# The first layer's up product of the last batch by Strassen's algorithm, its weight sums made one batch earlier

## Chip, cores and metric

One core of a Trainium2 chip runs the whole program. The metric is the device time of one execution in microseconds (us). Its engines are PE (TensorE, matrix products), DVE (VectorE), ACT (ScalarE), POOL (GpSimd) and SP (SyncE, which here only issues DMAs).

## The reference

Three stages are fused, each fed by the one before.

```python
# 1 linear attention: batch 4, heads 8, S 576, head width 64
q_p, k_p = phi(q), phi(k)
num = einsum('bhsf,bhfd->bhsd', q_p, einsum('bhsf,bhsd->bhfd', k_p, v))
x = num / (einsum('bhsf,bhf->bhs', q_p, k_p.sum(2))[..., None] + 1e-06)   # as 2304 x 512
# 2 first layer: w_in 512 x 2048, w_out 2048 x 512
h = x @ w_in
x = np.maximum(0.01 * h, h) @ w_out
# 3 second layer: 4 experts, w1 512 x 1024, w2 1024 x 512
out = sum(p[:, e:e+1] * (np.maximum(x @ w1[e], 0) @ w2[e]) for e in range(4))
```

The change touches `h = x @ w_in`, for the last of the four batches (576 of the 2304 rows).

## The kernel before

Every float32 operand of a matrix product is split in two parts, high and low (`hilo`, L120 to L125: ACT casts the high part, DVE subtracts it from the source and keeps the rest). A product takes three passes, high with high, high with low and low with high:

```python
    PASS = ((0, 0), (0, 1), (1, 0))
```

**The first layer.** Batches 0 to 3 are worked one after the other. The attention of batch b leaves x^T as KK = 4 tiles of 128 x 576 (`xh`, `xl`). The 2048 columns of w_in are taken 128 at a time: F counts these pieces through all batches, 16 per batch (NF), so batch 3 is F = 48 to 63. `moe1_up(F, n)` makes one half n (288 of the 576 columns) of piece F with 4 x 3 = 12 matmuls (L530). After both halves the gate follows: ACT writes 0.01 h (`hs`, L542), DVE takes the maximum (`g`, L544), ACT casts it (`gt`, L124), DVE makes its low part (L125). `moe1_down(C, d, n)` multiplies the four gated pieces of a group by w_out: 4 x 3 matmuls for each half n of each of the four output tiles d (L563). DVE adds the result to `acc` (L576); the first group of a batch is copied by ACT instead (L574).

**The order.** A group G holds GF = 4 pieces, so batch 3 is groups 12 to 15. In a group, ups of this group and downs of the one before alternate:

```python
ORDER = (("u", 0), ("d", 0), ("d", 1), ("u", 1), ("d", 2), ("d", 3), ("u", 2), ("u", 3))
```

Each "u" is 24 matmuls, each "d" 24. The order of the other work comes from a plan of steps with fractional batch times (`plan`, sorted). A scheduler then sets the order on each engine, save where the code calls `keep_in_program_order`. From the second batch on, weights are read back from float32 copies in DRAM: `w1_dma` loads a raw tile `wr` (128 x 512, 4 buffers), `w1_split` makes `wt` from it.

**What else runs in batch 3.** The second layer is already worked by Strassen's algorithm, in two blocks of tokens. `x2_steps(0)` and `x2_steps(1)` prepare its inputs from the finished batches: POOL makes differences (`xt`, L665), ACT casts (`xo`, L683), POOL subtracts (`xo`, L685), SP stores halves of them in DRAM (L692). `early()` loads `w1[1]` and `w2[0]` ahead. At the end of batch 3 SP loads `r`, the first expert's weights (L733), POOL makes their sums (`rs`, L747), ACT casts (`wuh`, L772) and POOL subtracts (`wul`, L777). Then PE starts the second layer's products (L849).

## Time and profile before

| What | Value |
|---|---|
| Median of 3 runs | 1342.0 us (1339.99 to 1342.63) |
| The profiled execution, its own time | 1342.56 us |
| Its span in the trace | 1340.8 us |
| PE busy | 1315.7 us (98%) |
| DVE, ACT, POOL busy | 69%, 48%, 49% |
| Up matmuls (L530), whole run | 1536, of which batch 3 has 384 |
| Batch 3's first layer, from F = 48 to the last `acc` | 502.7 to 618.9 us |

The trace has one row for each instruction or run of like instructions. A matmul's record is longer than the pace at which matmuls follow, because they overlap in the array; the pace is read from a run of them in the chain of waits.

### The profile page before, as it was taken

The page shows a single profiled execution, that of the slowest core. Times are in us where ns is not written, and L with a number is a line of the kernel's source. Part 1 is how long each engine was busy: PE and PEld are TensorE (multiplying, and loading weights), DVE is VectorE, ACT ScalarE, POOL GpSimd, SP SyncE. Part 2 cuts the span into 40 slices and gives each one's busy share as a digit, 9 for nine tenths or more (in the row PEclk, how much of TensorE's full clock was granted, in tenths as well). Part 3 has the DMA queues.
Part 4 walks back from the last instruction along what each step waited for, and adds up shares of the span by engine and source line. Part 5 has one row for each costly group of instructions (what it writes and reads, how often), then busy time and mean ns, then how long its engine had stood idle before and what let it go on. Part 6 is the DMA issues. An engine that isn't in the chain of part 4 may idle for free.

```text
span 1340.8 us, 23230 instructions
## 1 busy us (share of the span) xinstructions
PE 1315.7 (98%) x8303; PEld 1272.1 (95%) x8303; DVE 927.1 (69%) x1385; ACT 642.8 (48%) x1225; POOL 656.5 (49%) x550
## 2 busy tenths in 40 slices
PE   7979999999999999999999999999999999999998
PEld 6879999999999999999999999899999999999998
DVE  5589889877776665474666666556676667667667
ACT  5667656676666544543444444343333324332331
POOL 2223102111112103457566566278888868777775
PEclk9999999999999999999999999999999999999999
DMA  6465575433344234567999999998888899887882
GB/s 214 127 239 189 185 230 152 139 110 114 94 129 140 73 105 130 182 241 260 322 307 309 305 362 386 345 337 294 291 290 288 293 381 369 252 267 249 265 255 102
DMA packets 196850, 312.37 MB, mean 233 GB/s; under 512 B 20608, under 2 KB 96256, under 8 KB 196736
## 3 DMA queue, kind: packets, MB, share of 16 engines
q1 hardware_dynamic: 196736, 310.90, 70.4%
q8 instruction: 66, 1.08, 0.3%
q14 instruction: 48, 0.39, 0.1%
HBM read 222.04 MB, written 88.72 MB: 232 GB/s over the span
## 4 chain that ended last, share of the span: by engine, by line
PE 88%; DVE 6%; DMA 3%; issue 1%; ACT 1%; SPq 0%; DVEq 0%; ACTq 0%
PE po L1060 17%; PE op L563 13%; PE hp L530 12%; PE po L889 10%; PE py L1011 7%; PE px L1011 5%; PE pv L1011 5%; PE py L849 4%; PE kvp L258 3%; PE nm L351 3%; PE px L849 3%; PE pv L849 2%; PE pk L220 1%; DMA r<-w_in 1%; DVE gt L125 1%
## 5 line engine op out<-in xcount | busy, mean ns | idle before, releaser
L1076 DVE TENSOR_TENSOR ac<-po,ac 128x768 f32<-128x768 f32 x203 | 194.0, 956 | 123.7 <-PE po L1060 123.7
L1060 PE MATMUL po<-go,wo 128*128 128x384 f32 x1302 | 260.9, 336 | 0.0
L312 POOL PARTITION_ALL_REDUCE mb<-pc x32 | 78.0, 2440 | 347.8 <-ACT pc L310 258.6
L1060 PEld LDWEIGHTS po<-go,wo 128*128 128x128 f32 x1302 | 228.6, 188 | 0.4 <-ACT ac L1074 0.2
L563 PE MATMUL op<-gt,wt 128*128 128x288 f32 x1536 | 220.1, 297 | 1.7 <-DVE gt L125 1.5
L530 PE MATMUL hp<-xh,wt 128*128 128x288 f32 x1024 | 215.8, 297 | 1.4 <-DVE g L544 1.4
L563 PEld LDWEIGHTS op<-gt,wt 128*128 128x128 f32 x1536 | 208.1, 188 | 3.5 <-DVE gt L125 2.2
L1042 ACT CAST go<-t 128x384 fp32r<-128x384 f32 x124 | 63.8, 514 | 221.1 <-POOL t L1038 221.1
L530 PEld LDWEIGHTS hp<-xh,wt 128*128 128x128 f32 x1024 | 167.1, 188 | 2.8 <-DVE g L544 2.0
L530 PE MATMUL hp<-xl,wt 128*128 128x288 f32 x512 | 151.6, 296 | 1.8 <-DVE xl L125 1.8
L1046 POOL TENSOR_TENSOR go<-t,go 128x384 fp32r<-128x384 f32 x124 | 131.8, 1074 | 19.3 <-ACT go L1042 19.3
L889 PE MATMUL po<-wd,gh 128*128 128x512 f32 x384 | 129.8, 391 | 0.0
L1011 PE MATMUL py<-xo,wo 128*128 128x384 f32 x576 | 115.7, 336 | 0.0
L1046 POOL TENSOR_TENSOR go<-b,go 128x384 fp32r<-128x384 f32 x95 | 97.6, 1028 | 9.2 <-ACT go L1042 9.2
L1011 PEld LDWEIGHTS py<-xo,wo 128*128 128x128 f32 x576 | 101.3, 188 | 0.3
L530 PEld LDWEIGHTS hp<-xl,wt 128*128 128x128 f32 x512 | 96.1, 188 | 2.6 <-DVE xl L125 2.2
L907 DVE SCALAR_TENSOR_TENSOR ob<-po,pe,ob 128x512 f32<-128x512 f32 x90 | 67.4, 749 | 44.7 <-PE po L889 44.7
L1038 POOL TENSOR_TENSOR t<-b,b 128x384 f32<-128x384 f32 x62 | 64.0, 1032 | 62.2 <-DVE b L1031 62.2
L889 PEld LDWEIGHTS po<-wd,gh 128*128 128x128 f32 x384 | 72.0, 188 | 13.2
L125 DVE TENSOR_TENSOR wt<-wr,wt 128x512 fp32r<-128x512 f32 x96 | 72.0, 768 | 17.2 <-ACT wt L124 17.0
L1011 PE MATMUL px<-xo,wo 128*128 128x384 f32 x384 | 77.5, 337 | 0.0
L1011 PE MATMUL pv<-xo,wo 128*128 128x384 f32 x384 | 77.4, 337 | 0.0
(153 smaller groups left out, 2639.5 us busy)
## 6 DMA issues: line engine op xcount, KB each, us to landing
wo<-wu SPq DMA_DIRECT2D x224, 256.0 KB, 4.0
wo<-wx SPq DMA_DIRECT2D x124, 256.0 KB, 5.1
wo<-wp SPq DMA_DIRECT2D x97, 256.0 KB, 3.7
wr<-w SPq DMA_DIRECT2D x96, 256.0 KB, 2.8
r<-w SPq DMA_DIRECT2D x32, 512.0 KB, 5.7
wx<-ws SPq DMA_DIRECT2D x32, 512.0 KB, 5.1
wu<-wuh SPq DMA_DIRECT2D x16, 896.0 KB, 5.1
wu<-wul SPq DMA_DIRECT2D x16, 896.0 KB, 5.6
```

Of the source, the lines that this page charges most:

```text
L125: nc.vector.tensor_tensor(out=lo, in0=src, in1=hi.bitcast(F32), op=ALU.subtract)
L312: nc.gpsimd.partition_all_reduce(mb, pc, 128, bass_isa.ReduceOp.absmax)
L530: nc.tensor.matmul(hp[:, n, 0:HS], lhsT=wi[:, a, kk * 128 : (kk + 1) * 128], rhs=x[z][:, kk, n * HS : (n + 1) * HS], start=(kk == 0 and i ...
L563: nc.tensor.matmul(op[:, n, 0:HS], lhsT=wt1[1, C * GF + f][:, a, d * 128 : (d + 1) * 128], rhs=gts[C * GF + f][:, z, n * HS : (n + 1) * HS ...
L849: kept(nc.tensor.matmul(out, lhsT=ws[w][:, AOPS.index(a), kk * 128 : (kk + 1) * 128], rhs=x[z][:, kk], start=first and n == 0, stop=n == 5 ...
L889: kept(nc.tensor.matmul(op.rearrange("p (h m) -> p h m", h=2), lhsT=(gh, gl)[z][:, 2 * f + t, q : q + 128], rhs=d[:, w, f::2], start=n == ...
L907: kept(nc.vector.scalar_tensor_tensor(out=o, in0=op, scalar=ps, in1=o, op0=ALU.mult, op1=ALU.add))
L1011: kept(nc.tensor.matmul(out, lhsT=w[:, wz, kk * 128 : (kk + 1) * 128], rhs=x[z][:, kk], start=first and n == 0, stop=n == 5, skip_group_ch ...
L1038: kept(nc.gpsimd.tensor_tensor(out=t, in0=gr[k, a], in1=gr[k, b], op=ALU.subtract))
L1046: kept(eng.tensor_tensor(out=t[:, 1], in0=gr[k, name], in1=t[:, 0].bitcast(F32), op=ALU.subtract))
L1060: kept(nc.tensor.matmul(t[:, m, 0:TH], lhsT=w[:, wz, m * 128 : (m + 1) * 128], rhs=g[:, z], start=n == 0, stop=n == 2,))
L1076: kept(nc.vector.tensor_tensor(out=A[j, i], in0=src, in1=A[j, i], op=ALU.add))
```

## The change

In batch 3 (SB = 3) two pieces of w_in, a pair, are made together by Strassen's algorithm. The pair's weights are four blocks (two halves of the 512 inputs by two pieces), x^T of the batch is four blocks (two halves of the inputs by two halves of 288 columns). Seven products of 2 x 3 matmuls take the place of 48 matmuls: 42 per pair, 336 instead of 384 for the eight pairs (`pair_product`, L657 to L695 in the numbering of the changed kernel, its matmuls at L673).

What comes with it:

- Weight sums (`f_sums`, L554): in batch 2, four DVE operations of 128 x 256 per pair on the raw tiles (L564), and two DMAs that store them in DRAM (L567). In batch 3 `f_dma` (L575) loads seven forms of 128 KB per pair, `f_split` casts and subtracts each (256 columns). This replaces two loads of 256 KB and two casts and subtracts of 512 columns per pair.
- x forms (`x_mul_forms`, L407): four sums or differences and seven splits on 576 columns, where there were four splits.
- Sums of products, per pair: three ACT copies of 288 columns out of PSUM (L684, L686, L688) and two DVE adds in PSUM (L690, L693). The gate becomes one ACT leaky ReLU (L699) instead of ACT 0.01 h and DVE maximum.
- Downs of batch 3 in halves with one PSUM bank each, evicted by DVE 288 columns at a time, first group included (L806, L810).
- PE and ACT keep the program's order through batch 3 (`held`), from a list in `pair_group`. The steps of `x2_steps` go to 16 places of that list (`slot`).
- `early()` reuses the tile `xt` of `x2_steps(1)`, so its loads wait until POOL has read that tile. POOL now sums `w1[1]` before `r` (L988), and the load of `r` (L974) waits for a PE matmul 105 ahead of the next stage's first.
- POOL's first six differences (L906) wait for the last matmul of F = 47's up, whose `xl` gives their tile its place.

```diff
+SB = B - 1
+FORMS = ("a11", "s1", "s2", "a12", "s4", "s3", "a22")
+X2SLOTS = ((0,), (2, 1), (3, 5), (4,), (6, 8), (7,), (9, 10), (11,))
...
+    fwp = opened(leftw, "fwp", 7)
...
+    pin = {"on": ""}
+
+    def held(e, ins):
+        if e in pin["on"]:
+            tc.keep_in_program_order(ins)
...
+    def x_split(b, n, src):
...
+        nc.scalar.copy(out=hl[:, 0], in_=src)
+        nc.vector.tensor_tensor(out=hl[:, 1], in0=src, in1=hl[:, 0].bitcast(F32), op=ALU.subtract)
+
+    def x_mul_forms(b, hp):
...
+        if hp == 1:
+            t1 = unit("t1").rearrange("p (a s) -> p a s", a=2)
+            sub(t1, b12, b11)
+            x_split(b, "b11", b11)
+            x_split(b, "t1", t1)
+        if hp == NP - 1:
+            sub(b12, b22, b12)
+            sub(b11, b12, b11, ALU.add)
+            x_split(b, "t2", b11)
+            x_split(b, "b21", b21)
+            x_split(b, "b22", b22)
+            x_split(b, "t3", b12)
+            sub(b21, b21, b11)
+            x_split(b, "t4", b21)
...
+    def f_sums(F):
+        a, b = (raws1.pop((0, F - 1 + i)) for i in range(2))
+        t = [fwp.tile([128, 2, 256], F32, tag="fw", name="fs") for _ in range(2)]
+        s = {1: t[0][:, 0], 2: t[0][:, 1], 4: t[1][:, 0], 3: t[1][:, 1]}
+        for o, x, y, op in (
+            (1, b[:, 0:256], b[:, 256:512], ALU.add),
+            (2, s[1], a[:, 0:256], ALU.subtract),
+            (3, a[:, 0:256], b[:, 0:256], ALU.subtract),
+            (4, a[:, 256:512], s[2], ALU.subtract),
+        ):
+            nc.vector.tensor_tensor(out=s[o], in0=x, in1=y, op=op)
+        d = drw.tile([128, 4, 256], F32, name=f"fs_{F}")
+        for i in range(2):
+            nc.sync.dma_start(out=d[:, 2 * i : 2 * i + 2], in_=t[i])
...
+    def f_dma(F, a):
+        if F < B * NF:
+            t = wf[F, a] = fwp.tile([128, 2, 256], F32R, tag="fw", name="wf")
+            nc.sync.dma_start(out=t[:, 1].bitcast(F32), in_=wsum[F % NF][a]())
+
+    def f_split(F, a):
+        if F < B * NF:
+            t = wf[F, a]
+            hilo(t[:, 0], t[:, 1], t[:, 1].bitcast(F32), 'w', B)
...
+    PRODUCTS = {
+        1: ("a11", "b11"), 2: ("a12", "b21"), 3: ("s4", "b22"), 4: ("a22", "t4"),
+        5: ("s1", "t1"), 6: ("s2", "t2"), 7: ("s3", "t3"),
+    }
...
+        if F == SB * NF - 1:
+            pin["on"] = "A"
+            pair_product(F + 1, 1)
+            pin["on"] = ""
...
+    def pair_product(F, i):
...
+        for kk in range(2):
+            for wz, z in PASS:
+                held("P", nc.tensor.matmul(
...
+        if i == 1:
+            ub[F][1] = two("hp")
+            held("A", nc.scalar.copy(out=ub[F][1][:, 0, 0:HS], in_=X))
+        elif i == 5:
+            held("A", nc.scalar.copy(out=ss[:, 0], in_=V))
+        elif i == 6:
+            held("A", nc.scalar.copy(out=ss[:, 1], in_=Y))
+        elif i == 3:
+            held("V", nc.vector.tensor_tensor(out=V, in0=V, in1=ss[:, 1], op=ALU.add))
+            pair_gate(F, xv)
+        elif i == 7:
+            held("V", nc.vector.tensor_tensor(out=Z, in0=Y, in1=ss[:, 0], op=ALU.add))
+        elif i == 4:
+            pair_gate(F + 1, yz)
+
+    def pair_gate(F, t):
+        g = unit("g")
+        held("A", nc.scalar.activation(
+            out=g.rearrange("p (a s) -> p a s", a=2), in_=t[:, :, 0:HS], func=AF.Lrelu, alpha=0.01
+        ))
...
+    def pair_group(G):
...
+            if u == 0:
+                M += [
+                    P[1], f("a12="), P[4], w(F - 1), P[5], P[6], f("s4=", "s3="), d[0],
+                    f("a22=", "a11"), slot, P[2], f("s1"), d[1], f("s2"), P[3], slot, d[2], P[7],
+                    f("a12"), w(F), d[3], slot, d[4],
+                ]
+            else:
+                M += [
+                    P[1], P[4], f("s4="), w(F - 1), P[5], f("s3="), w(F), d[0], P[6], P[2],
+                    f("a22=", "a11"), d[1], f("s1"), slot, f("s2"), d[2], P[3], P[7],
+                ]
+        if (G + 1) * GF == B * NF:
+            M[-3:] = [P[3], P[7], d[2], lambda F=F: pair_product(F, 4)]
...
+        halves = "P" in pin["on"]
+        if halves:
+            op = one("op").unsqueeze(1).to_broadcast([128, 2, 512])
...
+        if c == 0 and halves:
+            held("V", nc.vector.tensor_copy(av, ov))
...
+                if F // NF == SB - 1 and F % 2:
+                    f_sums(F)
...
-                t = xp.tile([128, 3, 2, TH], F32, tag="x", name="xt")
+                if j:
+                    t = m2["early"] = accp.tile([128, 3, 2, TH], F32, tag="a", name="xt")
+                else:
+                    t = xp.tile([128, 3, 2, TH], F32, tag="x", name="xt")
...
     def early():
-        t = accp.tile([128, 2, 4, 256], F32, tag="a", name="r0")
+        t = m2["early"].rearrange("p a b c -> p (a b c)")[:, 0:2048]
...
-    plan += [(B - 0.1, lambda: r01.append(early()))]
-    plan += spread(x2_steps(0), B - 0.95, B - 0.5) + spread(x2_steps(1), B - 0.5, B - 0.05)
+    FB = SB * NF
+    plan += [(SB - 0.15 + 0.02 * i, lambda a=a: f_dma(FB, a)) for i, a in enumerate(FORMS)]
+    plan += [(SB - 0.08 + 0.02 * i, lambda a=a: f_split(FB, a)) for i, a in enumerate(FORMS[:3])]
+    plan += [(SB - 0.01, pair_feed)]
```

PE at the start of batch 3. `hp` on the left is an up, `op` a down; numbers tell the tiles apart. Before, the end of F = 48's up (`hp_5978`), then the first half down of group 11, which reads pieces 44 to 47 in turn (`gt_5850` is 47's):

```order
L530 MATMUL hp_5978<-xh_4805,wt_5855 128x288 x2
L530 MATMUL hp_5978<-xl_4806,wt_5855 128x288
L530 MATMUL hp_5978<-xh_4805,wt_5855 128x288
L563 MATMUL op_6013<-gt_5605,wt_5690 128x288 x3
L563 MATMUL op_6013<-gt_5709,wt_5789 128x288 x3
L563 MATMUL op_6013<-gt_5808,wt_5831 128x288 x3
L563 MATMUL op_6013<-gt_5850,wt_5884 128x288 x3
```

And now, from the end of F = 47's up (`hp_5905`) on: P1, P5 and P6 of the first pair, the same half down, then P2:

```order
L630 MATMUL hp_5905<-xh_3121,wt_5857 128x288
L673 MATMUL hp_5946<-xf_5220,wf_5744 128x288 x6
L673 MATMUL hp_5946<-xf_5220,wf_5777 128x288 x6
L673 MATMUL hp_5953<-xf_5843,wf_5792 128x288 x6
L792 MATMUL op_6002<-gt_5659,wt_5746 128x288 x3
L792 MATMUL op_6002<-gt_5774,wt_5879 128x288 x3
L792 MATMUL op_6002<-gt_5898,wt_5920 128x288 x3
L792 MATMUL op_6002<-gt_5957,wt_5976 128x288 x3
L673 MATMUL hp_5946<-xf_5843,wf_5820 128x288 x6
```

Between F = 47's up and the first down there were 24 matmuls, now there are 18. P5 writes the PSUM tile whose other bank P1 filled, and its first matmul waits for ACT's copy of P1.

DVE at the same place. Before, from the `g` of F = 47 on:

```order
L544 TENSOR_TENSOR g<-hp,hs 128x576 [waits Activation_49]
L125 TENSOR_TENSOR wt<-wr,wt 128x512 [waits DMAHW1_49,Activation_49]
L125 TENSOR_TENSOR gt<-g,gt 128x576 [waits Activation_49]
L125 TENSOR_TENSOR wt<-wr,wt 128x512 [waits DMAHW2_49,Activation_49]
L544 TENSOR_TENSOR g<-hp,hs 128x576 [waits Activation_49]
```

And now (`fs` are the sums of the last pair, `wf` low parts of forms; the third `fs` waits for P5's matmuls, since its tile is the buffer that P5 reads):

```order
L648 TENSOR_TENSOR g<-hp,hs 128x576 [waits Activation_49]
L564 TENSOR_TENSOR fs<-wr 128x256 [waits PE_49]
L564 TENSOR_TENSOR fs<-fs,wr 128x256 [waits DVE_49]
L564 TENSOR_TENSOR fs<-wr 128x256 [waits PE_49]
L136 TENSOR_TENSOR gt<-g,gt 128x576 [waits Activation_49]
L564 TENSOR_TENSOR fs<-wr,fs 128x256 [waits DVE_49]
L136 TENSOR_TENSOR wf<-wf 128x256 [waits DMAHW1_49,Activation_49]
L136 TENSOR_TENSOR wt<-wr,wt 128x512 [waits DMAHW3_49,Activation_49]
```

In both, the low part of `gt` of F = 47 comes first and the low part of `wt` of F = 47 later (the last `wt` row). Three sums now stand ahead of the one, and a fourth sum and a form between the two. The first half down reads both when it comes to piece 47.

SP in the middle of batch 3. Before, loads of `wr` between the stores of `xo`:

```order
L692 DMA xo_b_6543<-xo 128x768 [waits DMAHW1_49,Activation_49]
L692 DMA xo_b_6543<-xo 128x768 [waits DMAHW2_49,Pool_49]
L451 DMA wr<-w_0_13_1923 128x512 [waits DMAHW3_49,DVE_49]
L692 DMA xo_t_6633<-xo 128x768 [waits DMAHW4_49,Activation_49]
L692 DMA xo_b_6666<-xo 128x768 [waits DMAHW5_49,Activation_49]
```

And now:

```order
L933 DMA xo_b_6929<-xo 128x768 [waits DMAHW0_49,Activation_49]
L578 DMA wf<-fs_5755 128x256 [waits DMAHW1_49,PE_49]
L933 DMA xo_b_6929<-xo 128x768 [waits DMAHW2_49,Pool_49]
L578 DMA wf<-fs_5755 128x256 [waits DMAHW3_49,PE_49]
L578 DMA wf<-w_0_14_2055 128x256 [waits DMAHW4_49,DVE_49,PE_49]
L578 DMA wf<-w_0_13_1926 128x256 [waits DMAHW5_49,PE_49]
L578 DMA wf<-fs_5929 128x256 [waits DMAHW6_49,DVE_49,PE_49]
```

The loads of the forms (`wf`) stand behind stores that wait for POOL and ACT, and wait themselves for the PE product that last read their buffer.

## Rows read from the trace of the kernel before

**Rows 1.** The page's part 1: busy us, share of the span, instructions.

```profile
PE 1315.7 (98%) x8303; PEld 1272.1 (95%) x8303; DVE 927.1 (69%) x1385; ACT 642.8 (48%) x1225; POOL 656.5 (49%) x550
```

**Rows 2.** Chain of waits in batch 3: start us, us, what.

```profile
496.35 9.54 PE hp L530 x72
...
512.26 3.18 PE hp L530 x24
...
591.80 6.37 PE op L563 x48
```

**Rows 3.** Busy time by window: PE, PEld, DVE, ACT, POOL; clock, DMA share, GB/s.

```profile
440.00:480.00 40.00, 40.00 (x310) 40.00 (x309) 25.86 (x42) 20.68 (x41) 0.00 (x0) 1.00 0.30 87
560.00:600.00 40.00, 40.00 (x304) 40.00 (x303) 26.16 (x33) 18.49 (x29) 25.24 (x22) 1.00 0.61 211
```

**Rows 4.** ACT's groups, 380 to 640 us: shape, count | busy us, mean ns.

```profile
L124 ACT CAST gt<-g 128x576 fp32r<-128x576 f32 x32 | 21.6, 674 | 19.1 <-DVE g L544 19.1
L542 ACT ACTIVATE hs<-hp 128x576 f32<-128x576 f32 x32 | 20.8, 650 | 48.2 <-PE hp L530 48.1
L358 ACT COPY nf<-nm 128x288 f32<-128x288 f32 x12 | 4.7, 397 | 8.5 <-PE nm L351 8.5
```

**Rows 5.** DVE's groups, 380 to 640 us: the nearest to the new sums.

```profile
L819 DVE TENSOR_TENSOR ws<-r 128x256 f32<-128x256 f32 x4 | 1.6, 418 | 0.0
```

**Rows 6.** Timeline of DVE at F = 47: start us, us, instruction.

```profile
503.43 0.76 DVE L544 TENSOR_TENSOR g<-hp,hs 128x576 f32<-128x576 f32 x1 [0.92 <-ACT hs L542]
504.93 0.76 DVE L125 TENSOR_TENSOR gt<-g,gt 128x576 fp32r<-128x576 f32 x1
```

**Rows 7.** Timeline of DVE, low parts with POOL idle and with POOL busy.

```profile
497.11 1.89 DVE L125 TENSOR_TENSOR wt<-wr,wt 128x512 fp32r<-128x512 f32 x3
...
573.52 3.69 DVE L125 TENSOR_TENSOR wt<-wr,wt 128x512 fp32r<-128x512 f32 x3
577.13 0.74 DVE L544 TENSOR_TENSOR g<-hp,hs 128x576 f32<-128x576 f32 x1
...
578.62 1.50 DVE L125 TENSOR_TENSOR gt<-g,gt 128x576 fp32r<-128x576 f32 x1
```

**Rows 8.** Timeline of POOL, alone and in the stretch of rows 7.

```profile
518.44 1.99 POOL L685 TENSOR_TENSOR xo<-xt,xo 128x384 fp32r<-128x384 f32 x2 [6.97 <-ACT xo L683]
...
573.77 2.89 POOL L665 TENSOR_TENSOR xt<-xr,xt 128x384 f32<-128x384 f32 x2
```

**Rows 9.** Timeline of ACT: a cast that waits for DVE's result.

```profile
552.01 0.67 ACT L124 CAST gt<-g 128x576 fp32r<-128x576 f32 x1 [0.32 <-DVE g L544]
```

**Rows 10.** Timeline of PE, end of batch 3 and start of the next stage.

```profile
609.08 9.04 PE L563 MATMUL op<-gt,wt 128*128 128x288 f32 x66 [0.20 <-DVE gt L125]
...
618.97 0.61 PE L849 MATMUL px<-xo,wuh 128*128 128x384 f32 x2 [0.68 <-DVE acc L576]
...
620.13 0.52 PE L849 MATMUL pv<-xo,wuh 128*128 128x384 f32 x2
```

**Rows 11.** The page's part 6, DMA issues: count, KB each, us to landing.

```profile
wr<-w SPq DMA_DIRECT2D x96, 256.0 KB, 2.8
r<-w SPq DMA_DIRECT2D x32, 512.0 KB, 5.7
```

**Rows 12.** Timeline of POOL at the end of batch 3.

```profile
603.83 1.87 POOL L777 TENSOR_TENSOR wul<-r,wuh 128x768 fp32r<-128x768 f32 x1
...
607.68 1.94 POOL L747 TENSOR_TENSOR rs<-r 128x256 f32<-128x256 f32 x2
609.58 2.39 POOL L777 TENSOR_TENSOR wul<-rs,wuh 128x1024 fp32r<-128x1024 f32 x1
611.93 0.73 POOL L747 TENSOR_TENSOR rs<-rs,r 128x256 f32<-128x256 f32 x1
```

**Rows 13.** Timeline of SP's queue in batch 3: stores of xo that held it.

```profile
559.80 7.34 SPq L692 DMA_DIRECT2D xo_b<-xo  x2
...
585.20 12.46 SPq L692 DMA_DIRECT2D xo_t<-xo  x4
```

More of the change, by code (lines that the diff above doesn't have):

```diff
@@ L97, in opened @@
         )
-    left, left0, right, righte, leftl, psl = (ExitStack() for _ in range(6))
+    left, left0, leftw, right, righte, leftl, psl = (ExitStack() for _ in range(7))
     vp = opened(right, "vp", 2, side="right")
@@ L500, in w1_dma @@
         b, f = divmod(F, NF)
+        if i == 0 and b >= SB:
+            return
         if b == 0:
@@ L549, in moe1_up @@
         gts[F] = gt
+    ub = {}
+    def pair_product(F, i):
+        if i == 1:
+            ub[F] = [two("hp"), None, None]
+        elif i == 5:
+            ub[F][2] = unit("ss").rearrange("p (a s) -> p a s", a=2)
+        xv, yz, ss = ub[F]
+        X, V = xv[:, 0, 0:HS], xv[:, 1, 0:HS]
+        if yz is not None:
+            Y, Z = yz[:, 0, 0:HS], yz[:, 1, 0:HS]
+        out = {1: lambda: X, 2: lambda: X, 5: lambda: V, 3: lambda: V}.get(i, lambda: Y)()
+        a, b = PRODUCTS[i]
+        w, x = wf.pop((F, a)), xs[F // NF][b]
+        first = i in (1, 5)
+        n = 0
+        for kk in range(2):
+            for wz, z in PASS:
+                held("P", nc.tensor.matmul(
+                    out,
+                    lhsT=w[:, wz, kk * 128 : (kk + 1) * 128],
+                    rhs=x[z][:, kk],
+                    start=first and n == 0,
+                    stop=n == 5,
+                    skip_group_check=not first,
+                ))
+                n += 1
+        if i == 1:
+            ub[F][1] = two("hp")
+            held("A", nc.scalar.copy(out=ub[F][1][:, 0, 0:HS], in_=X))
+        elif i == 5:
+            held("A", nc.scalar.copy(out=ss[:, 0], in_=V))
[8 more added lines that the diff above has]
+            pair_gate(F + 1, yz)
@@ new lines, in pair_gate, with slot, pair_feed @@
+    def pair_gate(F, t):
+        g = unit("g")
+        held("A", nc.scalar.activation(
+            out=g.rearrange("p (a s) -> p a s", a=2), in_=t[:, :, 0:HS], func=AF.Lrelu, alpha=0.01
+        ))
+        gt = gp.tile([128, 2, S], F32R, tag="g", name="gt")
+        hilo(gt[:, 0], gt[:, 1], g, 'g', F // NF + 1)
+        gts[F] = gt
+    slots = []
+    def slot():
+        if slots:
+            for f in slots.pop(0):
+                f()
+    r01 = []
+    def pair_feed():
+        for j in range(2):
+            x = x2_steps(j)
+            slots.extend([x[i] for i in q] for q in X2SLOTS)
+        slots[-1].append(lambda: r01.append(early()))
@@ L568, in moe1_down @@
                     stop=(f == GF - 1 and i == 2),
-                )
-        if n == 0:
+                ))
+        if halves:
+            av, ov = accs[b][:, d, n * HS : (n + 1) * HS], op[:, n, 0:HS]
+        elif n == 0:
             return
-        av = accs[b][:, d].rearrange("p (a s) -> p a s", a=2)
-        if c == 0:
-            nc.scalar.copy(out=av, in_=op[:, :, 0:HS])
-        else:
-            nc.vector.tensor_tensor(out=av, in0=op[:, :, 0:HS], in1=av, op=ALU.add)
-        if c == NF // GF - 1:
+        else:
+            av, ov = accs[b][:, d].rearrange("p (a s) -> p a s", a=2), op[:, :, 0:HS]
+        if c == 0 and halves:
+            held("V", nc.vector.tensor_copy(av, ov))
+        elif c == 0:
+            held("A", nc.scalar.copy(out=av, in_=ov))
+        else:
+            held("V", nc.vector.tensor_tensor(out=av, in0=ov, in1=av, op=ALU.add))
+        if c == NF // GF - 1 and n == 1:
             nc.sync.dma_start(out=xd[b][:, d], in_=accs[b][:, d])
     def moe1_group(G):
+        if G >= SB * NF // GF and G < B * NF // GF:
+            return pair_group(G)
         def up(F, n):
```

93 lines of the change are left out of this document (80 added, 13 removed).

## The prediction, made before the changed kernel was run

> **What bounds the kernel now.** I read the page first: PE is busy 98% of the span [rows 1], so time goes down only where PE gets less work or waits less. Then the chain of waits: through batch 3 it holds nothing but PE's pieces, ups and downs without a gap [rows 2]. 24 up matmuls take 3.18 us, so one costs 132.6 ns, and a half down of 12 the same 1.59 us. Then the windows, for what the other engines have to spare: DVE is busy 25.9 of 40 us in batch 2 and 26.2 of 40 in the middle of batch 3, ACT 20.7 and 18.5, and POOL goes from nothing to 25.2 [rows 3]. So there is cover for more work on DVE and ACT, on average. What the average hides is where one of their results is needed at once, and there the timelines count.
>
> What follows is a sum against the profiled execution (1342.56 us, span 1340.8). The median of the three runs is 1342.0, 0.56 us lower, and the forecast is set against that. A measurement of this kernel can tell about 0.2% (2.7 us) from no change.
>
> **PE's saving.** 384 up matmuls of batch 3 become 336, of the same shape. 48 x 132.6 ns = **-6.4 us** [rows 2]. In this batch PE waits for nothing, so all of it shows unless a new wait comes in. Everything below is such waits.
>
> **First pair, the copy.** P5 follows P1 directly and waits for ACT's copy of P1. A copy of 288 columns out of PSUM takes 397 ns [rows 4]; with the last matmul's way out of the array (records of 297 ns at a pace of 133) that is about 0.6 us of idle PE. In all later pairs P4 of the pair before (six matmuls, 0.8 us) lies between P1 and P5, which covers it. **+0.6**, with little doubt.
>
> **First pair, DVE's line.** Set the end of F = 47's up to zero (502.7 us in the trace; the `g` of F = 47 starts at 503.43 and its low part ends at 505.69, so at 3.0 [rows 6]). Before, the first half down came to piece 47 after 24 + 9 matmuls, at 4.4. Now it does after 18 + 9, at 3.6, plus the 0.6 of the copy, and to the low weights three matmuls later: 4.4. On DVE the low part of that `wt` now stands behind `g`, four sums, the low part of `gt` and one form. Alone, these take: `g` ends at 1.5, three sums of 0.42 [rows 5] to 2.75, `gt` 0.76 to 3.5, a sum to 3.9, a form of 256 columns (as the sums, an estimate) to 4.35, `wt` 0.63 (497.11, three in 1.89 [rows 7]) to 5.0. PE then waits 0.5. That is the low end.
>
> The high end comes from POOL. POOL's six differences for the second layer are released by F = 47's last matmul, at this very moment. Three low parts that took 1.89 us with POOL idle took 3.69 with POOL at work on such differences, and a `gt` low part 1.50 where 0.76 is usual, while `g`, which reads PSUM, kept its 0.74 [rows 6, 7]. POOL's went from 1.0 to 1.45 each [rows 8], so six last 8.7 us and cover the whole line. At twice their time the seven operations behind `g` end at about 8.2 and PE waits 3.7. With the copy the first pair costs between 1.1 and 4.3. I take **+2.4 in all** (0.6 + 1.8), a little under the middle, because POOL's inputs are loaded late in batch 2 and may land after zero, which would spare the first of the seven.
>
> The Trainium skill, SBUF — State Buffer, section "SBUF: two separate sides", says that a DVE operation with two SBUF inputs and a GpSimd operation that reads SBUF hold a shared port pair in turn, and the loser is blocked for the whole instruction. By that rule DVE's line would take in POOL's six operations whole and the sum would come to 1345.6 (the last rival). The trace agrees in kind, not in size: in 3.69 us DVE did 1.89 us of work and POOL 2.5 of its own, more than turns allow.
>
> **Later groups.** At the start of groups 13, 14 and 15 the half down's fourth piece comes from P4 of the pair before. Between P4 and that matmul lie P5', P6' and nine matmuls: 21 x 0.1326 = 2.8 us. The gate needs ACT's ReLU (as `hs`, 0.65), the cast (0.67) [rows 4], the low part (0.76 [rows 6]) and the steps between engines (0.32 us is what ACT idles for a result of DVE [rows 9]): about 2.4 to 2.6. So 0 alone, up to 0.8 with the low part at 1.5. POOL is busy for two thirds of the middle of batch 3 [rows 3], but in pieces: **+0.6** for three, between 0 and 2.4.
>
> **Rest of batch 3.** Per pair ACT gets three copies (1.2), a gate, seven casts of 256 instead of two of 512, and loses `hs`, and DVE gets the eviction in halves; by the durations of rows 4 some 9 us (an estimate) of the 11.9 that PE needs for a pair and its downs, DVE about the same. Both keep up on average, and the chain of a result to its reader is long elsewhere (P2, P3, P7 stand a half down apart, 1.6 us): 0. The ReLU may need a table load on ACT. It falls between a gate and the next copy, over 5 us apart: 0.
>
> **Batch 2.** 32 sums of 0.42 us and about 5 us of form work go to DVE, 18 us over a batch of some 100 us in which it idles 14 in 40 [rows 3]. 4 MB of stores go out at a DMA share of 0.3. Bounds 0 and 1.5, since attention's own DVE chain could be pushed; I take **+0.2**, near the cover.
>
> **End of batch 3.** Before, PE waited 0.2 us for a low part ahead of the last 66 downs [rows 10]. Now P4's gate has 21 matmuls of cover, 2.8 us: **-0.2**. The last wait, 0.68 for `acc`, stays.
>
> **Next stage.** The load of `r` now waits for a PE matmul 105 ahead of the next stage, 13.9 us before the end of the downs, and lands 5.7 us later [rows 11]. Then POOL makes four sums of it (0.73 alone to 0.97 [rows 12]), 1.87 of low parts for the first product and 2.39 for the second. The second product starts 2.0 us after the downs (0.7 idle for `acc`, the rest the first product [rows 10]). With the sums of `w1[1]` done ahead: -13.9 + 5.7 + 2.9 + 4.3 = -1.0, no wait. If `w1[1]` itself lands as late, its four sums come first: 1.9 to 3.8, a wait of 0 to 1.8. Its tile is the one that POOL must first finish reading, so this is no remote case: **+0.4**, between 0 and 1.8.
>
> Sum: -6.4 + 2.4 + 0.6 + 0 + 0.2 - 0.2 + 0.4 = **-3.0 us**, 1339.6 against the profiled run, **1339.0** against the median.
>
> **Rivals.**
> *Nothing is lost but the copy and DVE's own time.* POOL's differences land late and DVE keeps up: -6.4 + 1.1 - 0.2 = -5.5, time 1336.5. For it: 14 us in 40 of idle DVE [rows 3]. Against: POOL's release at the same moment. Chance 0.23.
> *Given back.* The high ends hold, with half of the later groups: -6.4 + 4.3 + 1.2 + 1.8 + 0.2 - 0.2 = +0.9, time 1342.9; with all of them 1344.1. For it: rows 7. Against: POOL is busy in pieces. Chance 0.24.
> *Slower: SP holds the forms.* SP's queue is in order and was held for 7.34 and 12.46 us by stores of `xo` that waited for POOL and ACT [rows 13]. Now loads of forms stand behind such stores. The load of a form (P3's) is issued when its buffer is read, some 54 matmuls (7.2 us) before ACT's in-order cast of the next one; landing takes 2.8 for twice the size [rows 11]. That leaves 4.4 us. A hold of 12.46 would be 8 us late, the cast would stand at the head of ACT's line, and the copies behind it that P5 and P6 need would hold PE: -3.0 + 8 = +5.0, time 1347. The point from which it decides: holds that exceed the slack by 3.0 us in sum cancel the gain, by 5.7 make it slower by 0.2%. Against: those holds came where nothing behind them was needed soon, and the stores are now spread over 16 places. Chance 0.08.
> *Strict turns.* DVE's operations and POOL's six exclude each other for their whole length, as rows 7 and 8 would have it at the worst: six POOL operations of 1.0 are put into DVE's line, which ends at 5.0 + 6.0 = 11.0, and PE waits 6.6. With 0.6 for the copy and 0.8 x 3 later: -6.4 + 7.2 + 2.4 + 0.4 = +3.6, time 1345.6. For it: both engines' operations did get longer together. Against: three low parts of 0.63 beside POOL took 3.69, not the 4.4 that turns would take [rows 7, 8]. Chance 0.05. The SBUF — State Buffer page of the Trainium skill, as told above, would have it so.
>
> **The numbers.** Forecast band 1337.6 to 1341 with 0.40. The range reaches from the first rival to the second: 1335.8 to 1343.8. Faster by over 0.2% (below 1339.3) takes the first rival and 0.25 of the band: 0.48. Slower (above 1344.7) takes the last two: 0.13. The rest, 0.39, is the same.
>
> **What would show it.** L673 with 336 matmuls at 132 ns; one idle of PE of about 0.6 us for ACT's copy at the first P5; one for DVE's low part in the first half down of group 11, 0.5 to 3.7 us, with the sums at L564 near 0.42 or near 0.8; short waits on `gt` low parts at three group starts; a wait on POOL's low part at the second product of the next stage. I am wrong if PE idles in the middle of a pair, on `wf` or a copy, if SP's queue shows loads of forms held for more than 5 us ahead of such idles, or if batch 2 grows.

## The result: 0.6% slower, and the page after

The changed kernel takes 1349.7 us (median of 6 runs, 1347.78 to 1349.91) beside 1341.4 for the kernel before in the same session (6 runs, 1339.63 to 1342.85). The ratio is 1.006, with a 95% interval of 1.0047 to 1.0073. The forecast of 1339.0 was wrong in sign, and the time lies outside the range that was given. A second set of runs of the changed kernel (run 5 below) gave 1.0048 [1.0032, 1.0065].

The page of the changed kernel, part 1 (busy us, share of the span, instructions), which answers to [rows 1]:

```profile
PE 1316.4 (98%) x8255; PEld 1270.2 (94%) x8255; DVE 962.0 (71%) x1484; ACT 659.1 (49%) x1289; POOL 657.1 (49%) x550
```

48 matmuls are gone, as meant. DVE has 35 us more to do and ACT 16. PE's busy time has not fallen, though, so the page alone does not say where the time went. The starts of PE's matmuls do, cut at places that both traces have (times in us):

```
stretch                                                before     after
start to the up of F = 16 (batch 2 begins)             217.56    217.76   +0.2
to the first P1 (before: the up of F = 48)             284.98    286.44   +1.5
to the first px product of the next stage              116.43    121.26   +4.8
from there to the end                                  721.81    722.42   +0.6
span                                                  1340.78   1347.88   +7.1
```

The spans differ by 7.1 us and the medians by 8.3, because the profiled execution of the kernel before took 1342.56, 1.2 above its median.

The third line is batch 3. It holds 864 matmuls before and 816 now, and one of the next stage's. At the pace of [rows 2], 132.6 ns, these need 114.7 us and 108.3. So PE lost 1.7 us against its pace before and 12.9 now: the 6.4 saved are there, and 11.2 of new losses are put against them. Of the 12.9, 6.0 fall in the first 12 us, 4.5 between there and 108 us, and 2.4 at the end.

PE's timeline in the changed kernel (start us, us, instruction, in brackets the idle time before it and what ended it), all of batch 3's rows with idle time, and the first three of the next stage's:

```profile
505.62 1.86 PE L673 MATMUL hp<-xf,wf 128*128 128x288 f32 x12 [0.47 <-ACT hp L684]
510.42 0.40 PE L792 MATMUL op<-gt,wt 128*128 128x288 f32 x1 [1.63 <-DVE gt L136]
512.50 0.61 PE L792 MATMUL op<-gt,wt 128*128 128x288 f32 x1 [1.68 <-DVE wt L136]
535.52 1.85 PE L673 MATMUL hp<-xf,wf 128*128 128x288 f32 x12 [0.27 <-ACT hp L684]
566.29 0.53 PE L673 MATMUL hp<-xf,wf 128*128 128x288 f32 x2 [0.93 <-ACT wf L135]
567.56 0.80 PE L673 MATMUL hp<-xf,wf 128*128 128x288 f32 x4 [0.74 <-DVE wf L136]
586.52 1.86 PE L673 MATMUL hp<-xf,wf 128*128 128x288 f32 x12 [0.26 <-ACT hp L684]
614.03 10.24 PE L792 MATMUL op<-gt,wt 128*128 128x288 f32 x75 [0.56 <-DVE gt L136]
625.21 0.41 PE L1164 MATMUL py<-xo,wuh 128*128 128x384 f32 x1 [0.94 <-DVE acc L810]
632.55 0.44 PE L1086 MATMUL py<-xo,wuh 128*128 128x384 f32 x1 [0.66 <-DVE pz L1204]
633.19 0.45 PE L1086 MATMUL py<-xo,wuh 128*128 128x384 f32 x1 [0.19 <-DMA xo<-xo_t]
```

**The first pair.** 0.47 is the copy of P1. The two longest waits are the low parts that the prediction's term on DVE's line speaks of, in the first half down's piece 47. DVE's timeline there:

```profile
505.08 0.76 DVE L648 TENSOR_TENSOR g<-hp,hs 128x576 f32<-128x576 f32 x1 [0.92 <-ACT hs L642]
505.75 0.83 DVE L564 TENSOR_TENSOR fs<-wr 128x256 f32<-128x256 f32 x1
506.62 1.13 DVE L564 TENSOR_TENSOR fs<-fs,wr 128x256 f32<-128x256 f32 x1
507.67 1.24 DVE L564 TENSOR_TENSOR fs<-wr 128x256 f32<-128x256 f32 x1
508.83 1.54 DVE L136 TENSOR_TENSOR gt<-g,gt 128x576 fp32r<-128x576 f32 x1
510.29 1.22 DVE L564 TENSOR_TENSOR fs<-wr,fs 128x256 f32<-128x256 f32 x1
511.43 0.41 DVE L136 TENSOR_TENSOR wf<-wf 128x256 fp32r<-128x256 f32 x1
511.77 0.68 DVE L136 TENSOR_TENSOR wt<-wr,wt 128x512 fp32r<-128x512 f32 x1
```

And POOL's, in the same stretch:

```profile
504.32 1.98 POOL L906 TENSOR_TENSOR xt<-xr,xr 128x384 f32<-128x384 f32 x2 [78.45 <-PE hp L630]
506.25 2.37 POOL L906 TENSOR_TENSOR xt<-xr 128x384 f32<-128x384 f32 x2
508.58 2.64 POOL L906 TENSOR_TENSOR xt<-xr,xt 128x384 f32<-128x384 f32 x2
```

POOL starts with the end of F = 47's up, at 504.32, and its six differences last until 511.22. In just that time DVE's sums take up to 1.24 us instead of 0.42, and the low part of `gt` 1.54 instead of 0.76. The first two rows behind POOL's end are back at 0.41 and 0.68. `g`, which reads PSUM, kept its 0.76 with POOL at work.

What PE does behind the second wait was not in the prediction at all. Windows of PE's clock (us, PE, PEld, DVE, ACT, POOL, granted clock, DMA share, GB/s), the stretch right after it and the next one:

```profile
512.35:515.77 3.42, 3.27 (x13) 3.27 (x14) 2.23 (x7) 0.41 (x1) 0.00 (x0) 0.50 0.90 278
...
516.00:520.00 4.00, 4.00 (x32) 4.00 (x31) 1.71 (x4) 2.56 (x4) 0.00 (x0) 1.00 0.47 154
```

For 3.4 us the granted clock is 0.50, the lower level (1.2 GHz). 13 matmuls start where the pace would have some 26: about 1.7 us lost. So the 6.0 us are 0.6 (the copy), 3.7 (the two waits) and 1.7 (clock), each by how far the next matmul's start falls behind the pace.

**The rest of batch 3.** DVE is the engine that has filled up. Windows over the stage, before and then after:

```profile
503.00:618.00 115.00, 114.80 (x863) 114.23 (x861) 64.72 (x84) 53.82 (x86) 53.39 (x48) 1.00 0.56 187
```

```profile
505.00:625.00 120.00, 112.57 (x812) 109.51 (x810) 87.76 (x149) 70.75 (x148) 60.22 (x55) 0.99 0.61 201
```

64.7 us of 115 became 87.8 of 120. DVE's groups in batch 3 (count | busy us, mean ns | idle before), first two of the changed kernel, the first of them its largest item, then the one that `wf` and `wt` replace, before:

```profile
L136 DVE TENSOR_TENSOR wf<-wf 128x256 fp32r<-128x256 f32 x53 | 30.1, 595 | 5.2 <-ACT wf L135 5.0
...
L136 DVE TENSOR_TENSOR wt<-wr,wt 128x512 fp32r<-128x512 f32 x17 | 15.5, 909 | 0.0
```

```profile
L125 DVE TENSOR_TENSOR wt<-wr,wt 128x512 fp32r<-128x512 f32 x30 | 24.2, 826 | 7.8 <-ACT wt L124 7.7
```

A form's low part has a mean of 595 ns, but that mean mixes two kinds. By the timelines of DVE and POOL, 35 of the 53 met no instruction of POOL and took 416 ns, and the 18 that overlapped one took 943. A low part of `wt` has a mean of 909 ns against 0.63 us alone [rows 7]; 826 before, so POOL slowed this line before the change too. The chain of waits (start us, us, what) shows two ways in which this line and the forms reach PE; the first piece leads to the idle time at 535.52, the second to those at 566.29 and 567.56:

```profile
527.94 4.13 DMA wf<-fs
...
532.53 0.51 DVE wf L136
533.04 0.37 DVE acc L810
533.41 0.38 DVE hp L690
...
533.82 0.66 ACT g L699
...
535.08 0.40 ACT hp L684
...
535.52 1.85 PE hp L673 x12
...
557.32 8.49 DMA wf<-fs
...
565.84 0.41 ACT wf L135
...
566.27 1.24 DVE wf L136
```

Both begin with the load of a form. In the first, the form's low part and an eviction then stand ahead of the sum in PSUM (L690) that the gate needs, and ACT's next copy stands behind the gate. In the second, a form lands late, and then its low part takes 1.24 us; this one place costs 2.2 us of the 4.5.

**Batch 2.** Of its 1.5 us, 1.1 arise between the ups of F = 32 and F = 40. The ups of F = 34 and F = 36 alone lie 10.7 us apart before and 12.0 now, but most of that is no loss: 92 matmuls stand there instead of 84, and as many fewer in the stretches beside. The loss is in two waits for the gate that the kernel before does not have; with PE's slower start behind them they make up most of the 1.1 us. PE's timeline in the changed kernel:

```profile
412.36 0.38 PE L630 MATMUL hp<-xh,wt 128*128 128x288 f32 x1 [0.20 <-DVE g L648]
...
419.03 1.45 PE L792 MATMUL op<-gt,wt 128*128 128x288 f32 x9 [0.38 <-DVE g L648]
```

DVE's timeline ahead of the first, before and then after:

```profile
406.05 0.76 DVE L125 TENSOR_TENSOR kl<-kraw,kh 128x576 fp32r<-128x576 f32 x1
406.73 0.75 DVE L544 TENSOR_TENSOR g<-hp,hs 128x576 f32<-128x576 f32 x1
```

```profile
406.12 0.45 DVE L133 CAST kh<-kraw 128x576 fp32r<-128x576 f32 x1
409.22 0.75 DVE L414 TENSOR_TENSOR xq<-nf,rb 64x576 f32<-64x576 f32 x1 [2.65 <-DMA rb<-dr]
...
411.46 0.76 DVE L648 TENSOR_TENSOR g<-hp,hs 128x576 f32<-128x576 f32 x1
```

What the rows show is a change of order: a product that waits for the load of `rb` now stands ahead of the gate, and DVE idles 2.65 us at the head of its line with the gate behind it. The size is not steady. In the trace of run 5, the same kernel, only one such wait is left (0.28 us) and batch 2 takes 0.5 us more than before, not 1.5.

### The profile page after: what moved, and what is told of

Read it like the earlier page. It is cut to its first block, busy times and chain, and to the rows that moved or that the text cites. A ratio compares the mean times of both kernels' runs of the same rounds, so it can differ in the third digit from the quotient of the medians.

```text
span 1347.9 us, 23406 instructions
## 1 busy us (share of the span) xinstructions
PE 1316.4 (98%) x8255; PEld 1270.2 (94%) x8255; DVE 962.0 (71%) x1484; ACT 659.1 (49%) x1289; POOL 657.1 (49%) x550
## 4 chain that ended last, share of the span: by engine, by line
PE 81%; DVE 8%; DMA 5%; ACT 2%; issue 2%; SPq 1%; POOL 0%; DVEq 0%; ACTq 0%; POOLq 0%
PE po L1297 17%; PE op L792 11%; PE po L1126 10%; PE hp L630 7%; PE py L1248 7%; PE px L1248 5%; PE pv L1248 5%; PE py L1086 4%; PE nm L362 3%; PE kvp L269 3%; PE pv L1086 2%; PE px L1086 2%; PE hp L673 1%; PE pk L231 1%; DMA wf<-fs 1%
## 5 line engine op out<-in xcount | busy, mean ns | idle before, releaser
L792 PE MATMUL op<-gt,wt 128*128 128x288 f32 x1536 | 224.9, 298 | 5.6 <-DVE gt L136 3.2
L630 PE MATMUL hp<-xh,wt 128*128 128x288 f32 x768 | 165.4, 301 | 1.0 <-ACT xh L135 0.8
L630 PEld LDWEIGHTS hp<-xh,wt 128*128 128x128 f32 x768 | 127.6, 191 | 2.1 <-ACT xh L135 1.0
L630 PE MATMUL hp<-xl,wt 128*128 128x288 f32 x384 | 115.2, 300 | 1.8 <-DVE xl L136 1.8
L630 PEld LDWEIGHTS hp<-xl,wt 128*128 128x128 f32 x384 | 73.3, 191 | 2.4 <-DVE xl L136 2.0
L1126 PE MATMUL po<-wd,gl 128*128 128x512 f32 x192 | 75.0, 390 | 0.0
```

Source lines behind the costliest of these rows:

```text
L630: nc.tensor.matmul(hp[:, n, 0:HS], lhsT=wi[:, a, kk * 128 : (kk + 1) * 128], rhs=x[z][:, kk, n * HS : (n + 1) * HS], start=(kk == 0 and i ...
L792: held("P", nc.tensor.matmul(op[:, n, 0:HS], lhsT=wt1[1, C * GF + f][:, a, d * 128 : (d + 1) * 128], rhs=gts[C * GF + f][:, z, n * HS : (n ...
L1126: kept(nc.tensor.matmul(op.rearrange("p (h m) -> p h m", h=2), lhsT=(gh, gl)[z][:, 2 * f + t, q : q + 128], rhs=d[:, w, f::2], start=n == ...
```

## The experiments

Times are medians. Ratios are to the kernel before, run on the same chip beside them (1341.0 to 1342.0), with a 95% interval. "Batch 3" is the third line of the table above, read from each run's trace (before 116.4, after 121.3). A trace is one execution; where that lies more than 1.5 us off its run's median, it is said.

**1. PE's saving alone.** In the kernel before, 48 up matmuls of batch 3 are left out and nothing is added:

```diff
+        nk = KK - 1 if F // NF == B - 1 and n == 0 else KK
-        for kk in range(KK):
+        for kk in range(nk):
-                    stop=(kk == KK - 1 and i == 2),
+                    stop=(kk == nk - 1 and i == 2),
```

> The kernel before, in which the first half of each up of batch 3 leaves out its last three of twelve matmuls (16 x 3 = 48, so h of batch 3 lacks a quarter of its sum there). Nothing else changes. Theory A (PE sets the pace of batch 3 and the saving is real): 6.4 us less than before, about 1335. Theory B (DVE, ACT or DMA would have set the pace anyway, so that PE's saving turns into waits): less than 3 us.

1334.0 us, 0.9944 [0.9928, 0.9961]; batch 3 takes 109.2. The saving is real, 7.2 us. In the traces batch 3 is 7.3 us shorter: 6.4 for the matmuls and 0.9 because less is lost at its end (0.8 instead of 1.7). What the change loses is what it adds.

**2. POOL later.** A tiny operation on POOL reads the low weights of piece 47, so that POOL's differences start when DVE's line is through:

```diff
+                    y = wt1[1, SB * NF - 1][:, 1, 0:6].bitcast(F32)
+                    y = y.rearrange("p (a b c) -> p a b c", a=3, b=2)
+                    kept(nc.gpsimd.tensor_tensor(out=t[:, :, :, 0:1], in0=y, in1=y, op=ALU.subtract))
```

> The changed kernel with one small POOL operation (128 x 6) ahead of the first differences, which reads the low weights of piece 47. So POOL starts when DVE's line of the first pair is done; DVE's, ACT's and PE's orders stay. Theory A (the first pair loses 1.8 + 1.95 us to DVE operations that POOL doubles, and 2 us more to the lower clock that follows): the sums take 0.42 us instead of 1.1 to 1.2, PE waits 0.5 to 0.8 for the low weights, the clock stays at 1.0, and 4 to 5.5 us come back, about 1345. Theory B (POOL's start is needed when it is, or the wait moves on): 0 to 1 us, with as much idle PE later in batch 3.

DVE's timeline of this run, three of the same rows:

```profile
503.03 0.42 DVE L564 TENSOR_TENSOR fs<-wr 128x256 f32<-128x256 f32 x1
...
504.33 0.75 DVE L136 TENSOR_TENSOR gt<-g,gt 128x576 fp32r<-128x576 f32 x1
...
505.67 0.69 DVE L136 TENSOR_TENSOR wt<-wr,wt 128x512 fp32r<-128x512 f32 x1
```

And its PE:

```profile
506.41 0.40 PE L792 MATMUL op<-gt,wt 128*128 128x288 f32 x1 [0.21 <-DVE wt L136]
```

That settles the first pair: without POOL beside it, DVE's line is through in 3.3 us instead of 6.7, the waits of 1.63 and 1.68 become one of 0.21 (the low end of the prediction's term said 0.5), and the clock does not fall. The first 12 us cost 1.2 instead of 6.0. Yet batch 3 still takes 120.3: other waits came in from 12 us on, which was not expected. The whole takes 1345.9, 1.0042 [1.0024, 1.0061], 2.4 to 3.8 us less than the two sets of the changed kernel; in this trace only 1.0 us of that lies in batch 3.

**3. One load and cast later** (s2 behind P7 in the second pair of a group), since it stood ahead of a copy that PE needs:

```diff
-                    f("a22=", "a11"), d[1], f("s1"), slot, f("s2"), d[2], P[3], P[7],
+                    f("a22=", "a11"), d[1], f("s1"), slot, d[2], P[3], P[7], f("s2"),
...
```

> The changed kernel with one cast moved: in the second pair of a group, the form s2 of the next pair is cast after P7 instead of after d1, so its load has 42 matmuls (5.6 us) from the end of P6 instead of 18 (2.4 us). Theory A (forms are late because their buffer is freed shortly before ACT's line wants them): the waits of PE for the copy of P1 at the starts of groups 13 and 15 go, 0.7 to 1.6 us less. Theory B (stores on SP's queue or a busy DMA make them late, whatever the place): no change within 0.5 us.

1346.1, 1.0037 [1.0024, 1.0051]. Batch 3 took 121.6 in the profiled execution, with the first pair's waits again at 1.63 and 1.67 and the clock at 0.50 for 6.8 us. So the trace shows no gain from the edit. The whole is nevertheless 2.2 to 3.6 us shorter than the two sets of the changed kernel (1.0048 and 1.006, with overlapping intervals). Differences of this size can come without a cause that the trace shows, so what runs 2 and 4 tell is read from their traces.

**4. Sums in place**, written over the raw tiles that they read, so that no sum waits for a buffer that P5 reads:

```diff
-        s = {1: t[0][:, 0], 2: t[0][:, 1], 4: t[1][:, 0], 3: t[1][:, 1]}
+        s = {1: b[:, 256:512], 2: a[:, 0:256], 4: a[:, 256:512], 3: b[:, 0:256]}
...
```

The second and third sum change places, and the stores and their readers follow.

> The changed kernel with the weight sums written over the raw tiles that they are made from, instead of into tiles of the forms' pool. The last pair's sums then need not wait for P1 and P5 and stand ahead of the first pair. Theory A: DVE's line of the first pair holds only the low part of gt, one form and the low part of wt; with POOL at work these end near 5.5 us after F = 47's up, PE waits about 1.2 us there instead of 3.6, and if the clock then holds, 3 to 5 us come back, about 1345.5; if it falls all the same, 2. Theory B (the sums are not what delays): within 1 us of 1349.7.

1346.2, 1.0037 [1.0023, 1.005]; batch 3 takes 117.0. PE's timeline has one wait where there were two:

```profile
510.24 0.40 PE L791 MATMUL op<-gt,wt 128*128 128x288 f32 x1 [1.57 <-DVE wt L136]
```

The clock did not fall behind it.

**5. The changed kernel again**, beside the next ones:

> The changed kernel once more, unchanged, beside the others of this call. About 1349.7 us if the first measurement holds, with PE waiting 1.8 and 1.9 us for the low parts of piece 47 and the clock at 0.5 for some microseconds after.

1348.4, 1.0048 [1.0032, 1.0065]; batch 3 121.4, with waits of 1.64 and 1.68 and 6.8 us at half clock. The pattern repeats.

**6. Experiments 2 and 4 together.**

> Sums written in place and POOL's first differences held until the low weights of piece 47 are there, both. Theory A (sums and POOL delay DVE's line of the first pair, each for its part): PE waits 0.6 us for the copy and 0 to 0.5 for the low weights, no clock fall, group 12 as short as group 13; 1 to 2 us less than the sums in place alone, about 1344.7. Theory B (the wait only moves on to the forms' loads): no gain on the sums in place alone (1346.2), idle PE for forms in the first 20 us.

1346.3, 1.0032 [1.002, 1.0044]; batch 3 takes 116.1, as long as before. The first 12 us cost 1.5. So 6.0 of the 6.4 us saved are still lost, most of them in the middle (5.4 between 12 and 108 us). In this trace, whose execution took 1344.5, 1.8 below the median, the kernel is slower outside of batch 3 alone. The next question was what holds PE in the middle. From here on this kernel is the base.

**7 and 8. Two edits of order on it.** Run 7 adds experiment 3. Run 8 also loads POOL's second raw half earlier and holds the order of these loads on SP:

> The same, and the cast of s2 after P7 in the second pair of each group. Theory A: the waits for the copy of P1 at the starts of groups 13 and 15 go, another 0.5 to 1.5 us, about 1343.7. Theory B: nothing.

> The same, and the two loads of the second block's raw inputs (768 KB each) no longer together at the start of group 14, but one in group 13 after P3 and one in its second pair, with SP's order of the forms' loads held. In the changed kernel a form of 128 KB that was issued right behind both took 8.5 us to land, and PE waited 1.1 + 0.9 us for it. Theory A (the bytes ahead of it make that load late): it lands in 3 to 5 us and 1.5 to 2 us come back, about 1342. Theory B (the loads of forms are late for their buffers): the wait stays, and held order on SP may cost 1 us more.

1347.0, 1.0033 [1.002, 1.0046], and 1350.1, 1.0059 [1.0035, 1.0083]; batch 3 116.0 and 119.3. Run 7 changes nothing beside run 6. Run 8 missed: the load still went out late, behind a store of `xo` that held SP 2.38 us, and POOL's differences then fell on another busy stretch of DVE.

**9 and 10. The forms' work taken out.** In run 9, pairs 2 to 8 use the first pair's forms: no loads, casts or low parts. Run 10 keeps the casts and low parts and leaves out the loads alone:

```diff
...
-        if F < B * NF:
-            t = wf[F, a] = fwp.tile([128, 2, 256], F32R, tag="fw", name="wf")
+        if SB * NF < F < B * NF:
+            wf[F, a] = wkeep[a]
+        elif F < B * NF:
+            t = wkeep[a] = wf[F, a] = fwp.tile([128, 2, 256], F32R, tag="fw", name="wf")
```

In run 9 alone, in the function that splits a form:

```diff
-        if F < B * NF:
+        if F <= SB * NF:
```

> Sums in place and POOL held, as before, and the second to eighth pair use the first pair's seven forms again: no loads of forms, no casts and no low parts for them in batch 3 (so 14 of the 16 pieces of h are made from other columns of w_in). What is left of the change's cost is then the first pair, batch 2 and the end. Theory A (PE waits in groups 13 to 15 come from forms that are fetched anew): the stretch from P1 to the next stage falls from 116 us to about 112, the run by some 4 us. Theory B (the waits come from the pinned order of ACT and from the downs' evictions): less than 1.5 us.

> The same, but ACT and DVE cast and subtract the forms of every pair as before, from the tile that is there; only the DMA loads are left out (the numbers of h are then meaningless for the second to eighth pair). If the loads' landing is what is late, this is as fast as the run without casts, within 1 us; if ACT's and DVE's work on the forms is, it is as slow as with loads. I expect two thirds of the gain from the loads.

Without any of it, 1342.1, 1.001 [1.0, 1.002], batch 3 113.0. With casts and low parts but no loads, 1347.5, 1.0046 [1.003, 1.0061], batch 3 117.4 (in an execution of 1344.9, 2.6 below the median). So ACT's and DVE's work on the forms costs 5.4 us, and no execution of run 10 is as short as the longest of run 9. It is not the loads, against what was expected: forms that land late are in the chain of the changed kernel, but without loads nothing is won.

**11. Batch 2.** The attention products there are planned 0.3 of a head pair later, to move the one that waits for `rb` (on run 7):

```diff
+                t += 0.3 if f is x_mul and b == SB else 0
```

> Sums in place, POOL held, s2 late, and the first two products that form x of batch 3 emitted a third of a head pair later, so that on DVE they stand behind two gates of batch 2 instead of ahead of one. In the changed kernel DVE stood 2.65 us at the head of its line for their operand from DRAM. Theory A (this and no lack of DVE time is what batch 2 loses): from piece 34 to piece 36 10.7 us as before the change instead of 11.7 to 12.9, the run 1 to 2.5 us shorter, about 1344.5. Theory B (the sums' time is): no change.

1348.0, 1.0057 [1.0041, 1.0072], no shorter than run 7. F = 34 to F = 36 fell to 9.8 us, but now holds 78 matmuls, so this tells nothing of the wait. DVE still idles for a load of the attention there (2.68 us for `ds`), and batch 2 as a whole took 286.5 us, beside 286.4 in the changed kernel and 288.2 in run 7. A miss: the edit moved the order on PE, and what a wait of DVE's line costs in batch 2 was not settled.

**12. A shorter low part.** From pair 2 on, DVE copies the high part instead (one input):

```diff
...
+                held("V", nc.vector.tensor_copy(t[:, 1], t[:, 0].bitcast(F32)))
```

> Sums in place and POOL held, loads and casts of all forms as they are, but from the second pair on DVE only copies a form's high part where it made the low part (one input in SBUF instead of two; h of batch 3 then has a wrong low part). It tells DVE's line from ACT's. Theory A (the low parts of forms, doubled by POOL, stand in DVE's line ahead of the sums in PSUM and the evictions that PE waits for): a copy takes 0.25 to 0.3 us beside POOL too, DVE is busy 70 us instead of 88 in batch 3, the stretch from P1 to the next stage falls from 116 to 113.5 us, near the run without casts (113). Theory B (ACT's line, with the casts, is what holds PE): it stays at 115 or more.

1344.9, 1.0028 [1.0018, 1.0037]; batch 3 116.9. DVE's timeline of this run:

```profile
520.64 1.10 DVE L586 CAST wf<-wf 128x256 fp32r<-128x256 f32 x1
...
523.08 0.28 DVE L586 CAST wf<-wf 128x256 fp32r<-128x256 f32 x1
```

A copy takes 0.28 alone and 0.9 to 1.1 beside POOL (49 have a mean of 556 ns). So DVE's busy time in batch 3 fell from 87.9 us in run 6 to 82.0, not to the 70 that was expected, and the run tells little on what a shorter line would bring.

**13 and 14. ACT's half and DVE's half.** On run 9: the casts alone, or the low parts alone (from resident tiles):

> As the run that keeps the first pair's forms (no loads), with ACT's casts of every pair's forms, but without DVE's low parts of them (h of batch 3 is then meaningless). Without both the stretch from P1 to the next stage took 113.0 us, with both 117.4. Theory A (DVE's line is what holds PE): 113 to 114. Theory B (ACT's line, pinned, is): 116 to 117.5. If the two lines hold each other, both runs of this pair lie between.

> The counterpart: DVE's low parts of every pair's forms, without ACT's casts. Theory A: 116 to 117.5 us. Theory B: 113 to 114.

1342.6, 1.0009 [1.0, 1.0018], batch 3 112.9 for the casts; 1344.4, 1.0022 [1.001, 1.0034], batch 3 117.8 for the low parts. The windows of batch 3, casts alone:

```profile
504.20:617.00 112.80, 110.48 (x818) 108.65 (x816) 58.78 (x97) 70.52 (x148) 59.13 (x56) 1.00 0.46 156
```

and low parts alone:

```profile
508.40:626.00 117.60, 113.52 (x818) 110.37 (x817) 89.67 (x146) 56.10 (x99) 63.04 (x56) 0.99 0.45 150
```

With ACT's load at 70.5 us and DVE's at 58.8 batch 3 is as short as with no form work; with DVE's at 89.7 it takes 4.8 us more. But 4.1 of these are one event, a wait of 2.14 us for a low part of `wt`, which stood in DVE's line as POOL's six differences of the second block began, and 3.4 us at half clock behind it; and the execution in the trace was the longest of ten, 1350.5, 6.1 above the median. So the trace shows that DVE's line can hold PE here, not that it does so as a rule. The whole times point the same way and are weaker: against the kernel before, neither half costs 1.1 us (run 9), the casts alone 0.9, the low parts alone 2.7 (the last two with overlapping intervals), both 6.5 (run 10). Why both halves together take 3 us longer than the low parts alone stays open. No run took POOL's differences out of the middle of batch 3, so how much of the forms' price is POOL's slowing of DVE, and how much only their place in the line, is not told apart.

**15. ACT's order freed** (on run 6; in the forms' part of the order PE alone stays in the written one):

```diff
-                pin["on"] = "PA"
+                pin["on"] = "P"
```

> Sums in place and POOL held, loads, casts and low parts as they are, but ACT's order in batch 3 is left to the scheduler; PE's stays. If the written order of ACT is what makes PE wait, the stretch from P1 to the next stage falls from 116.1 us to 114 or less and the run comes near the kernel before; if DVE's line is, it stays within 1 us, or grows.

1360.0, 1.0145 [1.0128, 1.0161]; batch 3 128.8. The written order on ACT is not the cause; the scheduler's is worse.

No version was found that beats the kernel before: even run 9, with nearly all of the forms' work gone, is no faster. In its trace batch 3 is 3.4 us shorter than before, and batch 2 and the next stage take 2.2 more.

## Why the prediction was wrong

- **PE's saving, -6.4: right.** Left out alone it gave 7.2 us, 0.9 of it from less lost at the end of batch 3.
- **The copy in the first pair, +0.6: right** (0.47 of idle time, 0.6 against the pace).
- **DVE's line in the first pair, +1.8: the first step that failed.** The choice went "a little under the middle, because POOL's inputs are loaded late in batch 2 and may land after zero". They did not: POOL started with the release. The high end, a wait of 3.7, came true to a tenth (DVE's line ended 8.1 after the end of the up, where it said 8.2). That it met so closely is in part luck. It had seven operations at about twice their time, beside POOL for 8.7 us; by its own numbers that ends at 8.3 (the ratio of rows 7) to 8.5 (twice). Measured, POOL was through at 6.9, five operations took 5.68 us where 2.44 is their time alone, and the last two took their time alone. Runs 2 and 4 confirm the mechanism: without POOL, or without the sums, the line is shorter and so is the wait. The fall of the clock behind these waits, 1.7 us more, had no term. The term 2.4 (with the copy) measured 6.0, outside its bounds.
- **Later groups, +0.6**: at the starts of groups 13, 14 and 15 there was no wait for a low part of `gt` but two of 0.26 and 0.27 for a copy that stood behind the gate. Against the pace these are 1.1 us: right in size at half of its upper bound, but another place.
- **Rest of batch 3, "Both keep up on average": 0, the second step that failed.** It cost some 3.4 us, 2.2 of them at the form that landed late. The estimate of some 9 us a pair held for ACT (70.75 us over eight pairs, 8.8 each), not for DVE "about the same": 87.8, or 11.0 each. It was a sum of durations without POOL beside them, and an average. Seven low parts a pair at 595 ns are 4.2 us, at 416 2.9, and sums in PSUM and evictions on which PE waits stand in the same line. Runs 9 and 10 show that the casts and low parts cost 5.4 us and the loads nothing that shows. Runs 13 and 14 point at DVE's half and do not prove it.
- **Batch 2, +0.2: too small in the profiled execution.** It measured 1.5 there, the upper bound, and 0.5 in run 5. The prediction looked for the amount of DVE's work; the rows show order, with a load's wait at the head of the line and the gate behind it. How much of the loss that is stays open.
- **End of batch 3, -0.2: wrong in sign, +0.7.** 0.56 for a low part of `gt` and 0.94 for `acc` (before 0.20 and 0.68 [rows 10]).
- **Next stage, +0.4: right in size, wrong in place** (+0.6). The low part by POOL came in time; the 0.19 is for `xo` from DRAM. The 0.66 for a DVE result is there before, too.

Of the rivals, "given back" has the mechanism that came true in the first pair, with its high end, and with half of the later groups' (1.2; 1.1 measured). Its 1342.9 is short by the clock, the rest of batch 3, batch 2 and the end, and has 1.2 too much for the next stage. "SP holds the forms" named a time near the measured one. Forms did land late in the trace, but run 10, without loads, is no faster, so the time was met for another reason. "Strict turns" priced the first pair at 7.2 with the copy; it measured 4.3 without the clock and 6.0 with it. Between 505.75 and 511.43 DVE did 2.4 us of work (four sums of 0.42 and 0.76). POOL's six operations, 6.0 us alone [rows 8], took 6.9, so in these 5.68 us POOL did some 4.9 of its own (an estimate): together more work than turns would let through. The Trainium skill, SBUF — State Buffer, section "SBUF: two separate sides", has the loser fully blocked; the trace again agrees in kind, with most of the loss DVE's, and not in size.

## What to carry to other kernels

Work moved to an engine with idle time must be costed in that engine's in-order line, at the durations that hold beside its neighbours: here DVE's share went from 56% to 73% of the stage, a quarter of it still idle, and the work on the forms, ACT's and DVE's together, cost 5.4 us (runs 9 and 10). What PE needs at once stands in the same lines. Where the profile has a row for the contended duration and nothing excludes the overlap, take that row, not a value between. Add to each new wait of PE the matmuls that may follow at the lower clock, and read the scheduler's new order also in the stage before, where a wait for a load can come to the head of a line.
